# Sinkhorn's tiles summed before its product, one turn for the shares of two passes, and the first scalings on ScalarE

## The chip, the cores and the metric

The kernel runs on one core of one Trainium2 chip. The metric is the time of one execution on the device in microseconds; lower is better. The kernel before has a median of 2116.34 us over three runs (2116.13 to 2116.73).

## The reference

A local attention with a few global keys feeds a mixture of eight experts. Attention: batch 4, 8 heads, 768 positions, 64 columns a head; its output is read as x, 3072 tokens by 512 columns. The experts: layer one is 512 to 1024, layer two 1024 to 512, and every token passes through all eight. The weight P of each expert for each token is made by eight rounds of Sinkhorn:

```python
logits = x @ w_gate                       # 3072 x 8
P = np.exp(logits - logits.max())
for _ in range(8):
    P /= P.sum(1, keepdims=True) + 1e-09  # over the experts of a token
    P /= P.sum(0, keepdims=True) + 1e-09  # over all tokens, for each expert
    P *= N / E
for e in range(E):
    out += P[:, e:e + 1] * (np.maximum(x @ w1[e], 0.0) @ w2[e])
```

All is float32.

## The kernel before

**The stages.** First the attention, with a part of expert 0 computed in the background. Then pass 0 of the experts over the last third of the tokens (1024 of 3072, eight tiles of 128), in which the weights are prepared and written to DRAM as they are used; then passes 1 and 2 over the other two thirds, which read the prepared weights back. The cut falls near 264 us (end of attention) and 910 us (end of pass 0) of the profile.

**Pass 0** is a loop over 31 groups g of two 128-wide blocks of hidden units: three groups of expert 0 (its first block pair was done in the background), then four for each of experts 1 to 7. Each turn of the loop computes the first layer of group g (`layer1_strassen`, 42 products of 512 columns into the PSUM banks a, b, c, d), prepares the weights of a later group on ScalarE and GpSimd, and computes the second layer of group g - 1 (`second`, lines 1192 to 1213: eight tiles of 512 columns, six products each, in three PSUM banks `y_ps`). VectorE adds each tile into an accumulator `acc` (in the trace a part of the tile `early`): without a weight for expert 0 (line 1204), with the share P as a per-row scale for the others (line 1210). Before the first group of expert 1 is added, the eight accumulator tiles are multiplied by the share of expert 0: `first_scaled`, lines 1206 to 1209, four on VectorE (i = 1) and four on ScalarE (i = 0). This is done in the turn g = 4, for group 3.

**Sinkhorn** (`sinkhorn`, lines 913 to 943) works on `pm`, 128 partitions by 24 token tiles by 8 experts, so that a token is a partition and a tile. A round sums over the experts on VectorE (line 934), divides (935 to 937), and then needs a sum over all tokens: a product with a 128 x 128 matrix of ones sums over partitions for all 192 columns and spreads the result to every partition (line 939), and VectorE sums its 24 tiles from PSUM (line 940) before it divides (941 to 943). It is a generator, and `beat()`, called at places in the first and second layers, moves it on by one step, so that its products are traced between those of the first groups.

**The shares of passes 1 and 2.** There the tokens lie along the free dimension, so the share of an expert is needed as a row, spread over partitions. `spill_rows` (lines 1179 to 1185) turns the shares: in each of the turns g = 7, 8, 9 and 10 four transposes of a 128 x 8 block of `pm` go to one PSUM tile `pr_ps`, ScalarE copies 8 x 512 to `prow`, and a DMA writes it to `p_rows` in DRAM. `load_share` (line 1161) reads rows of it back, the first time near 900 us.

**What sets the order.** Each engine runs its instructions in a fixed order. A planner sets this order while the program is built, from its own estimate of when inputs and buffers are there: an instruction that is ready sooner may be issued ahead of ones traced before it. Instructions that go through `Ordered` or `InOrder` (lines 51 and 108) stay in the order of the program: TensorE from the turn g = 4 on (`moe.pe = attention.pe`, line 1242; all of those have line 115 or 118 in the profile), not before, and Sinkhorn's own products not. ScalarE's and SyncE's work in pass 0 is free from the turn g = 1 on.

Of the kernel before, what the change touches and what calls it, by code (L numbers as in the profile page):

```python
# [8 lines left out]
F32 = mybir.dt.float32  # L9
# [3 lines left out]
ALU = mybir.AluOpType  # L13
AX = mybir.AxisListType
# [3 lines left out]
P = 128  # L18
# [4 lines left out]
EPS = 1e-9  # L23
UT = 3
UNIT = UT * P
WT = 4
WIDE = WT * P
# [541 lines left out]
class Moe:  # L569
# [343 lines left out]
    def sinkhorn(self, ps, tag):  # L913

        nc, E, N = self.nc, self.E, self.N
        TT = N // P
        lg, pm, ones, small = self.lg, self.pm, self.ones, self.small
        gm = small.tile([P, 1], F32, name="gm")
        nc.vector.tensor_reduce(out=gm, in_=lg.rearrange("p t e -> p (t e)"), op=ALU.max, axis=AX.X)
        yield  # L920
        gmt_ps = ps.tile([P, P], F32, name="gmt_ps", tag=tag)
        self.pe.transpose(out=gmt_ps[0:1], in_=gm, identity=self.ident)
        gmax = small.tile([1, 1], F32, name="gmax")
        nc.vector.tensor_reduce(out=gmax, in_=gmt_ps[0:1], op=ALU.max, axis=AX.X)
        yield
        ngm_ps = ps.tile([P, 1], F32, name="ngm_ps", tag=tag)
        self.pe.matmul(ngm_ps, lhsT=ones[0:1, :], rhs=gmax, start=True, stop=True)
        nc.vector.tensor_scalar(out=gm, in0=ngm_ps, scalar1=-1.0, scalar2=None, op0=ALU.mult)
        nc.scalar.activation(out=pm, in_=lg, func=AF.Exp, bias=gm, scale=1.0)
        cols = TT * E  # L930
        for _ in range(SINKHORN_ITERS):
            bank = ps.tile([P, cols + TT + E], F32, name="c_ps", tag=tag)
            c_ps, rsum, csum = bank[:, 0:cols], bank[:, cols:cols + TT], bank[:, cols + TT:]
            nc.vector.tensor_reduce(out=rsum, in_=pm, op=ALU.add, axis=AX.X)
            nc.vector.tensor_scalar(out=rsum, in0=rsum, scalar1=EPS, scalar2=None, op0=ALU.add)
            nc.vector.reciprocal(out=rsum, in_=rsum)
            nc.vector.tensor_tensor(out=pm, in0=pm, in1=rsum.unsqueeze(2).broadcast_to([P, TT, E]), op=ALU.mult)
            yield
            self.pe.matmul(c_ps, lhsT=ones, rhs=pm, start=True, stop=True)
            nc.vector.tensor_reduce(out=csum, in_=c_ps.rearrange("p (t e) -> p e t", e=E), op=ALU.add, axis=AX.X)  # L940
            nc.vector.tensor_scalar(out=csum, in0=csum, scalar1=EPS, scalar2=float(E) / N, op0=ALU.add, op1=ALU.mult)
            nc.vector.reciprocal(out=csum, in_=csum)
            nc.vector.tensor_tensor(out=pm, in0=pm, in1=csum.unsqueeze(1).broadcast_to([P, TT, E]), op=ALU.mult)


def pipeline(tc, attention, ident, moe, acc, scratch):
# [4 lines left out]
    nc = tc.nc  # L951
    KT, KH, DM, NU, E = moe.KT, moe.KH, moe.DM, moe.NU, moe.E
    BT = 2 * WT
    NB = NU * UT // BT
# [4 lines left out]
    with ExitStack() as top:  # L959
# [9 lines left out]
        p_rows = dram.tile([E, NB - 1, 2, WIDE], F32, name="p_rows")  # L969
# [10 lines left out]
        NG = len(groups)  # L980
        xs = []
        for u in range(NU):
            c = u * UT % RT
# [109 lines left out]
        sps = first.enter_context(tc.tile_pool(name="sps", bufs=1, space=PSUM, reuse_waits="tile"))  # L1093
# [32 lines left out]
        def beat():  # L1126
            next(sinkhorn, None)
# [6 lines left out]
        passes = [NB - 1] + list(range(NB - 1))  # L1134
        FULL = DM // 2

        def spill_weights(g):

            w = wts[g]
            if g < NG - 1:  # L1140
                if g:
                    w2_sums[g] = w2pool.tile([P, 4, FULL], F32, name="w2sum", bufs=1)
                    moe.winograd_sums(w, w2_sums[g])
                t = moe.winograd_blocks(w2_sums[g], w2pool)
            to = w_spill[g] = dram.tile([P, 14, 2, FULL], F32R, name=f"ws{g}")
            dma(to[:, 0:7], w[0], sync if g == 0 else nc.sync)
            if g == NG - 1:
                for f in range(FG):
                    for s in range(2):
                        dma(to[:, 7 + 2 * f:9 + 2 * f, s], w[1][:, s, f].rearrange("p (d c) -> p d c", d=2))  # L1150
                return
            dma(to[:, 10], w[1][:, :, 1, 0:FULL])
            for d in range(2):
                dma(to[:, 12 + d], w[1][:, :, 0, d * FULL:(d + 1) * FULL])
            dma(to[:, 7:10], t[:, 0:3])
            dma(to[:, 11], t[:, 3])
# [19 lines left out]
                for m in range(lo, hi):  # L1176
                    blocks_of[0, 0, m] = t[:, m - lo]

        def spill_rows(p, i):

            bank = sps.tile([P, WT, P], F32, name="pr_ps", tag="s")
            for t in range(WT):
                moe.pe.transpose(out=bank[0:E, t], in_=moe.pm[:, passes[p + 1] * BT + 2 * t + i], identity=ident)
            nc.scalar.copy(out=prow[0:E], in_=bank[0:E].rearrange("p t c -> p (t c)"))
            nc.sync.dma_start(out=p_rows[:, p, i], in_=prow[0:E])

        def reload(p, ms=FIRST_BLOCKS):
            for m in ms:
# [3 lines left out]
        def second(g, hs, halves=(0, 1)):  # L1192
            e, b = groups[g][0], passes[0]
            first_scaled = e != 0 and groups[g - 1][0] == 0
            for i in halves:
                for t in range(WT):
                    j = 2 * t + i
                    tt = b * BT + j
                    y_ps = moe.layer2(t, wts[g], hs[i], yps, "y")
                    if t == 2:  # L1200
                        beat()
                    a = acc[:, j]
                    if e == 0:
                        nc.vector.tensor_tensor(out=a, in0=y_ps, in1=a, op=ALU.add)
                    else:
                        if first_scaled and i:
                            nc.vector.tensor_scalar(out=a, in0=a, scalar1=moe.pm[:, tt, 0:1], scalar2=None, op0=ALU.mult)
                        elif first_scaled:
                            nc.scalar.mul(a, a, moe.pm[:, tt, 0:1])
                        nc.vector.scalar_tensor_tensor(out=a, in0=y_ps, scalar=moe.pm[:, tt, e:e + 1], in1=a,  # L1210
                                                       op0=ALU.mult, op1=ALU.add)
                    if g == NG - 1:
                        nc.sync.dma_start(out=moe.out[tt * P:(tt + 1) * P, :], in_=a)

        for j in list(range(1, BT - UT, 2)) + list(range(0, BT - UT, 2)):
            u, t = divmod(passes[0] * BT + j, UT)
# [8 lines left out]
        def pieces_of_last(n):  # L1225
            for _ in range(n):
                next(last, None)
# [12 lines left out]
        for g in range(NG):  # L1240
            if prev is not None and groups[prev[0]][0] > 0:
                moe.pe = attention.pe
            to = ring_set if g == 0 else ring_set[0:2] + pool_set[2:4] if g == 1 else (pool_set, ring_set)[g % 2]
            hs = moe.layer1_strassen(ops, wts[g], to, tmp, mps, "h", g == 0, first_beat if g == 0 else beat)
            if g == 0:
                pieces_of_last(2 * UT)
                fill.close()
                w2pool = first.enter_context(tc.tile_pool(name="w2pool", bufs=2, side="right", reuse_waits="tile"))
                hpool = first.enter_context(tc.tile_pool(name="hpool", bufs=1))
                h_set = hpool.tile([P, 8, WIDE], F32R, name="h_set")  # L1250
                prow = hpool.tile([P, WIDE], F32, name="prow")
                pool_set += [(h_set[:, n], h_set[:, n + 1]) for n in range(0, 8, 2)]
                second(g, hs, (1,))
                moe.plain_blocks(wts[1])
            spill_weights(g)
            if g + 1 < NG and g + 1 not in wts:
                wts[g + 1] = moe.strassen_pair(moe.strassen_stage(*moe.stage_pair(*groups[g + 1], stage), stage),
                                               wpools[(g + 1) % 2])
                moe.plain_blocks(wts[g + 1])
            if 0 <= g - NG // 4 < 2 * (NB - 1):  # L1260
                spill_rows(*divmod(g - NG // 4, 2))
            if g == NG - 1:
                reload(1)
            if g == 1:
                second(*prev, (0,))
                second(g, hs, (0,))
                moe.act = nc.scalar
            elif g == 2:
                second(*prev, (1,))
            elif prev is not None:  # L1270
                second(*prev)
            prev = (g, hs)
# [146 lines left out]
def kernel(  # L1419
# [40 lines left out]
    with tc.If(rv > 0) as cmp:  # L1460
        pipeline(tc, band, ident, moe, acc, scratch)
# [34 lines left out]
```

## Time and profile before

| | us |
|---|---|
| median of three runs | 2116.34 (2116.13 to 2116.73) |
| the profiled execution, its own time | 2116.03 |
| span of its profile, first to last instruction | 2114.2 |
| TensorE busy | 2098.1 (99%) |
| GpSimd, VectorE, ScalarE busy | 1518.1, 1327.0, 725.6 |

The profile names engines PE (TensorE's products), PEld (its weight loads), DVE (VectorE), ACT (ScalarE), POOL (GpSimd) and SP (SyncE, which issues the DMAs). A row of a timeline has the start in us from the first instruction, the duration, the engine, the line of the kernel, the operation, output and inputs, shapes, count, and in brackets the idle time before and what ended it. The duration of one product includes the part in which the next already runs, so the pace of products is read from their starts.

### The profile page before, as it was taken

The page shows a single profiled execution, that of the slowest core. Times are in us where ns is not written, and L with a number is a line of the kernel's source. Part 1 is how long each engine was busy: PE and PEld are TensorE (multiplying, and loading weights), DVE is VectorE, ACT ScalarE, POOL GpSimd, SP SyncE. Part 2 cuts the span into 40 slices and gives each one's busy share as a digit, 9 for nine tenths or more (in the row PEclk, how much of TensorE's full clock was granted, in tenths as well). Part 3 has the DMA queues.
Part 4 walks back from the last instruction along what each step waited for, and adds up shares of the span by engine and source line. Part 5 has one row for each costly group of instructions (what it writes and reads, how often), then busy time and mean ns, then how long its engine had stood idle before and what let it go on. Part 6 is the DMA issues. An engine that isn't in the chain of part 4 may idle for free.

```text
span 2114.2 us, 30105 instructions
## 1 busy us (share of the span) xinstructions
PE 2098.1 (99%) x10505; PEld 1737.7 (82%) x10505; DVE 1327.0 (63%) x2368; ACT 725.6 (34%) x1487; POOL 1518.1 (72%) x1338
## 2 busy tenths in 40 slices
PE   8999999999999999999999999999999999999998
PEld 6888888888888888888888888888788888888886
DVE  7777667656566665655666556656746665566556
ACT  7777634323233332223222222222232222222221
POOL 5977969776777877347767677677577767777675
PEclk9999999999999999999999999999999999999999
DMA  7777487566666656776566565666956566566564
GB/s 168 211 208 207 145 298 295 217 235 223 240 235 223 244 214 244 246 281 210 184 213 208 187 209 182 218 206 218 357 186 208 185 211 212 177 204 212 189 207 149
DMA packets 235043, 458.04 MB, mean 217 GB/s; under 512 B 106465, under 2 KB 167905, under 8 KB 215169
## 3 DMA queue, kind: packets, MB, share of 16 engines
q1 hardware_dynamic: 234880, 456.01, 63.3%
q8 instruction: 85, 1.39, 0.3%
q14 instruction: 78, 0.63, 0.1%
HBM read 313.80 MB, written 142.15 MB: 216 GB/s over the span
## 4 chain that ended last, share of the span: by engine, by line
PE 94%; DVE 3%; POOL 1%; DMA 1%; issue 1%; ACT 0%; SPq 0%; DVEq 0%; ACTq 0%; POOLq 0%
PE c_acc L115 26%; PE y_ps L115 16%; PE bank_c L115 11%; PE bank_a L115 11%; PE bank_d L115 11%; PE bank_b L115 5%; PE t_ps L118 2%; PE o_ps L115 2%; PE s_ps L115 2%; PE h_ps L115 1%; PE o_t L115 1%; DVE early L1357 1%; PE tp L118 1%; PE y_ps L876 1%; PE y_ps L875 1%
## 5 line engine op out<-in xcount | busy, mean ns | idle before, releaser
L1353 DVE TENSOR_TENSOR early<-early,c_acc 128x512 f32<-128x512 f32 x308 | 210.2, 687 | 174.8 <-PE c_acc L115 174.8
L59 POOL TENSOR_TENSOR early<-full,full 128x512 f32<-128x512 f32 x56 | 72.8, 1300 | 291.0 <-DVE full L762 291.0
L59 POOL TENSOR_TENSOR full<-full,full 128x512 f32<-128x512 f32 x174 | 227.1, 1305 | 0.3
L1210 DVE SCALAR_TENSOR_TENSOR early<-y_ps,pm,early 128x512 f32<-128x512 f32 x224 | 167.5, 749 | 84.2 <-PE y_ps L115 83.9
L115 PE MATMUL bank_c<-x,wb 128*128 128x512 f32 x732 | 185.8, 389 | 0.0
L115 PE MATMUL bank_a<-m,wb 128*128 128x512 f32 x732 | 185.7, 389 | 0.0
L115 PE MATMUL bank_d<-x,wb 128*128 128x512 f32 x732 | 185.7, 389 | 0.0
L115 PEld LDWEIGHTS bank_a<-m,wb 128*128 128x128 f32 x732 | 137.4, 188 | 28.5
L115 PEld LDWEIGHTS bank_d<-x,wb 128*128 128x128 f32 x732 | 137.4, 188 | 28.5
L115 PEld LDWEIGHTS bank_c<-x,wb 128*128 128x128 f32 x732 | 137.4, 188 | 28.6
L115 PE MATMUL y_ps<-w,x 128*128 128x512 f32 x672 | 155.1, 389 | 0.6 <-DVE early L1210 0.6
L115 PE MATMUL y_ps<-w,h_set 128*128 128x512 f32 x672 | 154.8, 389 | 0.0
L115 PEld LDWEIGHTS y_ps<-w,x 128*128 128x128 f32 x672 | 125.9, 188 | 27.1 <-DVE early L1210 1.1
L115 PEld LDWEIGHTS y_ps<-w,h_set 128*128 128x128 f32 x672 | 126.0, 188 | 26.1
L773 DVE TENSOR_TENSOR early<-early,bank_d 128x512 f32<-128x512 f32 x62 | 42.6, 687 | 152.5 <-PE bank_d L115 152.3
L115 PE MATMUL c_acc<-x,wb 128*128 128x512 f32 x540 | 137.0, 389 | 0.0
L622 POOL TENSOR_TENSOR w<-w1f,w 128x256 fp32r<-128x256 f32 x62 | 44.9, 743 | 122.0 <-ACT w L621 122.0
L115 PEld LDWEIGHTS c_acc<-x,wb 128*128 128x128 f32 x540 | 101.3, 188 | 21.1
L643 POOL TENSOR_TENSOR wsum<-w1f 128x256 f32<-128x256 f32 x155 | 109.4, 741 | 9.1 <-DMA w1f<-in_moe_w_dram 9.1
L59 POOL TENSOR_TENSOR x<-full,x 128x512 fp32r<-128x512 f32 x90 | 115.9, 1324 | 0.0
L765 ACT CAST x<-full 128x512 fp32r<-128x512 f32 x90 | 56.0, 623 | 161.9 <-POOL full L59 135.9
L359 ACT ACTIVATE p_sb<-p_sb,mx 128x256 f32<-128x256 f32 (+1 forms) x192 | 92.5, 483 | 41.0 <-DVE mx L355 40.4
(375 smaller groups left out, 5063.4 us busy)
## 6 DMA issues: line engine op xcount, KB each, us to landing
wb<-ws SPq DMA_DIRECT2D x123, 1024.0 KB, 6.7
wb<-ws SPq DMA_DIRECT2D x121, 768.0 KB, 4.2
ws<-w SPq DMA_DIRECT2D x31, 1792.0 KB, 5.7
ws<-w SPq DMA_DIRECT2D x94, 256.0 KB, 2.5
ws<-w2s SPq DMA_DIRECT2D x30, 768.0 KB, 5.3
w1f<-in_moe_w_dram SPq DMA_DIRECT2D x32, 512.0 KB, 4.1
w2f<-in_moe_w_dram SPq DMA_DIRECT2D x32, 512.0 KB, 4.5
x<-op_m SPq DMA_DIRECT2D x16, 512.0 KB, 9.5
```

The costliest lines, as they stand in the source:

```text
L59: return lambda *args, **kw: self.tc.keep_in_program_order(op(*args, **kw))
L115: return self.tc.keep_in_program_order(self.engine.matmul(*args, **kw))
L118: return self.tc.keep_in_program_order(self.engine.transpose(*args, **kw))
L359: nc.scalar.activation(out=pv, in_=pv, func=AF.Exp, bias=mx[:, u:u + 1], scale=-1.0, accum_out=sm[:, i, j:j + 1])
L622: self.nc.gpsimd.tensor_tensor(out=lo, in0=full, in1=hi, op=ALU.subtract)
L643: nc.gpsimd.tensor_tensor(out=s[:, n], in0=x, in1=y, op=op)
L765: nc.scalar.copy(out=ops[k][:, 0], in_=src)
L773: tt(out=t3, in0=t3, in1=d, op=ALU.subtract)
L875: self.pe.matmul(y_ps, lhsT=hh[:, cols], rhs=lf, start=(f == 0), stop=False)
L876: self.pe.matmul(y_ps, lhsT=hl[:, cols], rhs=wf, start=False, stop=False)
L1210: nc.vector.scalar_tensor_tensor(out=a, in0=y_ps, scalar=moe.pm[:, tt, e:e + 1], in1=a, op0=ALU.mult, op1=ALU.add)
L1353: nc.vector.tensor_tensor(out=sums[k][q], in0=sums[k][q], in1=bank, op=ALU.add)
```

## The change

1. In each round of Sinkhorn VectorE sums the 24 tiles first, from SBUF, into a new tile `part` of 128 x 8. The product with the ones then has 8 columns and not 192, and the division reads its result from PSUM directly; the sum that stood behind the product is gone. The number of VectorE instructions is the same.
2. `spill_rows` is called once, in the turn g = 7. Two ScalarE copies bring the shares of both passes into a new tile `pcol`, 128 x 128, in the order (expert, pass, half, tile); one transpose of 128 x 128 turns them, one ScalarE copy of 128 x 128 takes them to `prow`, and one DMA writes all 128 rows. Before there were 16 transposes, four copies and four DMAs in four turns.
3. All eight first scalings go to ScalarE.

```diff
@@ sinkhorn @@
-        cols = TT * E
+        part = small.tile([P, E], F32, name="c_part")
         for _ in range(SINKHORN_ITERS):
-            bank = ps.tile([P, cols + TT + E], F32, name="c_ps", tag=tag)
-            c_ps, rsum, csum = bank[:, 0:cols], bank[:, cols:cols + TT], bank[:, cols + TT:]
+            bank = ps.tile([P, TT + 2 * E], F32, name="c_ps", tag=tag)
+            c_ps, rsum, csum = bank[:, 0:E], bank[:, E:E + TT], bank[:, E + TT:]
             nc.vector.tensor_reduce(out=rsum, in_=pm, op=ALU.add, axis=AX.X)
             nc.vector.tensor_scalar(out=rsum, in0=rsum, scalar1=EPS, scalar2=None, op0=ALU.add)
             nc.vector.reciprocal(out=rsum, in_=rsum)
             nc.vector.tensor_tensor(out=pm, in0=pm, in1=rsum.unsqueeze(2).broadcast_to([P, TT, E]), op=ALU.mult)
+            nc.vector.tensor_reduce(out=part, in_=pm.rearrange("p t e -> p e t"), op=ALU.add, axis=AX.X)
             yield
-            self.pe.matmul(c_ps, lhsT=ones, rhs=pm, start=True, stop=True)
-            nc.vector.tensor_reduce(out=csum, in_=c_ps.rearrange("p (t e) -> p e t", e=E), op=ALU.add, axis=AX.X)
-            nc.vector.tensor_scalar(out=csum, in0=csum, scalar1=EPS, scalar2=float(E) / N, op0=ALU.add, op1=ALU.mult)
+            self.pe.matmul(c_ps, lhsT=ones, rhs=part, start=True, stop=True)
+            nc.vector.tensor_scalar(out=csum, in0=c_ps, scalar1=EPS, scalar2=float(E) / N, op0=ALU.add, op1=ALU.mult)
...
@@ pipeline @@
-        def spill_rows(p, i):
-
-            bank = sps.tile([P, WT, P], F32, name="pr_ps", tag="s")
-            for t in range(WT):
-                moe.pe.transpose(out=bank[0:E, t], in_=moe.pm[:, passes[p + 1] * BT + 2 * t + i], identity=ident)
-            nc.scalar.copy(out=prow[0:E], in_=bank[0:E].rearrange("p t c -> p (t c)"))
-            nc.sync.dma_start(out=p_rows[:, p, i], in_=prow[0:E])
+        def spill_rows():
+
+            row = pcol.rearrange("q e p i t -> q (e p i t)")
+            for p in range(NB - 1):
+                first_tile = passes[p + 1] * BT
+                nc.scalar.copy(out=pcol[:, :, p], in_=moe.pm[:, first_tile:first_tile + BT].rearrange("q (t i) e -> q e i t", i=2))
+            bank = sps.tile([P, P], F32, name="pr_ps", tag="s")
+            moe.pe.transpose(out=bank, in_=row, identity=ident)
+            nc.scalar.copy(out=prow, in_=bank)
+            nc.sync.dma_start(out=p_rows.rearrange("e p i (t c) -> (e p i t) c", c=P), in_=prow)
...
-                        if first_scaled and i:
-                            nc.vector.tensor_scalar(out=a, in0=a, scalar1=moe.pm[:, tt, 0:1], scalar2=None, op0=ALU.mult)
-                        elif first_scaled:
+                        if first_scaled:
                             nc.scalar.mul(a, a, moe.pm[:, tt, 0:1])
...
-                prow = hpool.tile([P, WIDE], F32, name="prow")
+                prow = hpool.tile([P, P], F32, name="prow")
+                pcol = hpool.tile([P, E, NB - 1, 2, WT], F32, name="pcol")
...
-            if 0 <= g - NG // 4 < 2 * (NB - 1):
-                spill_rows(*divmod(g - NG // 4, 2))
+            if g == NG // 4:
+                spill_rows()
```

## The prediction, made before the result was known

> **What bounds the kernel now.** I read the engines' totals first, then TensorE's own waits in the stretch that the change touches, then that stretch turn by turn, then single rows. The totals and the chain of waits:
>
> ```profile
> PE 2098.1 (99%) x10505; PEld 1737.7 (82%) x10505; DVE 1327.0 (63%) x2368; ACT 725.6 (34%) x1487; POOL 1518.1 (72%) x1338
> ...
> PE 94%; DVE 3%; POOL 1%; DMA 1%; issue 1%; ACT 0%; SPq 0%; DVEq 0%; ACTq 0%; POOLq 0%
> ```
>
> TensorE is busy for 99% of the span and is 94% of the chain that ends last. So an edit pays only in TensorE time that it takes away, or in a wait of TensorE that it ends. In 255 to 520 us, where all of the change lies, the list of TensorE's waits has one row:
>
> ```profile
> PE y_ps L115 <- DVE early L1210: 0.6, 1, 0.6
> ```
>
> The stretch in windows, each one turn of the loop (columns: window, length, busy time and instructions of each engine, granted clock, DMA share, GB/s):
>
> ```profile
> 345.95:367.66 21.71, 21.07 (x94) 17.14 (x93) 16.75 (x27) 8.96 (x14) 18.94 (x19) 1.00 0.74 288
> ...
> 388.06:408.46 20.40, 20.40 (x92) 16.90 (x91) 12.55 (x18) 6.64 (x10) 15.39 (x15) 1.00 0.62 231
> 408.46:429.34 20.88, 20.88 (x96) 17.17 (x95) 12.64 (x18) 7.10 (x11) 15.87 (x15) 1.00 0.63 237
> 429.34:450.20 20.86, 20.86 (x96) 17.16 (x95) 12.64 (x18) 7.10 (x11) 15.38 (x15) 1.00 0.65 228
> 450.20:471.07 20.87, 20.87 (x96) 17.16 (x95) 12.58 (x18) 7.11 (x11) 15.46 (x15) 1.00 0.62 228
> 471.07:491.93 20.86, 20.86 (x96) 17.16 (x95) 12.59 (x18) 7.10 (x11) 15.37 (x15) 1.00 0.63 227
> ```
>
> A turn with nothing of the change in it is 20.40 us: 90 products, 0.2267 each. The four turns with transposes are 20.88 + 20.86 + 20.87 + 20.86 = 83.47, which is 1.87 above four plain turns. The turn from 345.95 is 1.31 above one; it holds the last round of Sinkhorn and the wait. These excesses, and seven more rounds of Sinkhorn before 345.95, are all that the change can win on TensorE.
>
> **Part 1, the product of 8 columns.** What a round costs now, from starts on TensorE (the last two rows are the weight loads behind the pair; all float32 products here are two instructions):
>
> ```profile
> 281.60 0.39 PE L710 MATMUL bank_a<-m,w 128*128 128x512 f32 x1
> 281.82 0.49 PE L939 MATMUL c_ps<-pm,ones 128*128 128x192 f32 x2
> 281.99 0.19 PEld L708 LDWEIGHTS bank_c<-x,w 128*128 128x128 f32 x1
> 282.15 0.19 PEld L709 LDWEIGHTS bank_c<-x,w 128*128 128x128 f32 x1
> 282.38 0.40 PE L709 MATMUL bank_c<-x,w 128*128 128x512 f32 x1
> ```
>
> From 281.60 to 282.38 TensorE does one product of 512 columns, the pair, and another such product; less 2 x 0.2267 the pair takes 0.33. A weight load is issued when the product before it begins, so the loads at 281.99 and 282.15 put each half at 0.165. Eight rounds are 8 x 0.33 = 2.6.
>
> No row shows a full-width pair of 8 columns. The nearest:
>
> ```profile
> 262.47 0.35 PE L907 MATMUL gt_ps<-ident,g_sb 16*128 16x16 f32 x3
> 262.75 0.19 PEld L710 LDWEIGHTS h_ps<-x,w1h 128*128 128x128 f32 x1
> 262.86 0.19 PEld L708 LDWEIGHTS h_ps<-x,w1h 128*128 128x128 f32 x1
> ...
> 276.35 0.38 PE L927 MATMUL ngm_ps<-gmax,ones 1*128 1x1 f32 x2
> 276.66 0.50 PE L890 MATMUL y_ps<-w2h,hh 128*128 128x512 f32 x1
> ```
>
> Three products of 16 columns take 262.75 - 262.47 = 0.28, so 0.093 each, and the weight load behind them, with no long product to hide it, holds the array for 262.86 - 262.75 = 0.11. A pair of one column takes 276.66 - 276.35 = 0.31. So weights decide, not columns: behind a product of 8 columns the next load lies bare. The first load of a pair still hides behind a product of 512, the second and that of the next product do not: 2 x 0.11 = 0.22. I take that, since the 16-column row is nearest in width: saved 0.33 - 0.22 = 0.11 a round, 0.9 in all. Bounds: the one-column pair (0.02 a round, 0.2 in all) and a pair that costs nothing (2.6).
>
> [...]
>
> On VectorE a round keeps its eight instructions; one sum moves ahead of the product:
>
> ```profile
> L934 DVE TENSOR_REDUCE c_ps<-pm x8: 349/360/363, 277.9 to 343.9; 128x24 f32<-128x192 f32 x8
> L937 DVE TENSOR_TENSOR pm<-pm,c_ps x8: 343/353/355, 279.3 to 345.6; 128x192 f32<-128x192 f32 x8
> L940 DVE TENSOR_REDUCE c_ps<-c_ps x8: 353/356/367, 282.3 to 350.9; 128x8 f32<-128x192 f32 x8
> ```
>
> The sum removed is 0.356; the new one, from SBUF, is closest to line 934, 0.360 (with a stride, so perhaps a little more). That it lies ahead of the product costs nothing: the first division ends at 279.3 + 0.35 = 279.65 and its product starts at 281.82, 2.2 later; the last ends at 345.95, its product is the 16th of that row, after 350. TensorE never waited for one. Were that cover gone, it would be 8 x 0.36 = 2.9.
>
> **Part 2, one turn for the shares.** 1.87 over 16 transposes is 0.117 each. The new one has 128 columns of weights and not 8; the nearest row is eight transposes of the attention with a product behind them:
>
> ```profile
> 251.16 1.09 PE L118 MATMUL t_ps<-ident,p_sb 128*128 128x128 f32 x8
> ...
> 252.01 0.48 PE L115 MATMUL y_ps<-w2l,hh 128*128 128x512 f32 x1
> ```
>
> (252.01 - 251.16) / 8 = 0.106 each, so wide weights are no dearer. One alone, with its change to and from the other products, I take as 0.15: saved 1.72 (bounds 1.6 and 1.77). Fifteen transposes, three DMA issues on SP and a copy less; p_rows is not read before 900 us, so neither the later single DMA nor its smaller rows lie on anything.
>
> What is added is a wait: the transpose needs two ScalarE copies, where the old ones needed only pm. Behind it on TensorE, in program order, are the 48 products of the second layer. When ScalarE does the copies is the planner's choice:
>
> ```profile
> 397.69 0.71 ACT L621 CAST w<-w1f 128x256 fp32r<-128x256 f32 x2
> 409.88 0.59 ACT L845 COPY early<-bank_c 128x512 f32<-128x512 f32 x1 [0.26 <-PE bank_c L115]
> ...
> 420.82 0.58 ACT L715 ACTIVATE x<-bank_a 128x512 fp32r<-128x512 f32 x1
> 421.31 1.04 ACT L679 CAST w2s<-w2sum 128x1024 fp32r<-128x1024 f32 x1
> ...
> L929 ACT ACTIVATE pm<-lg,gm x1: 457/457/457, 277.3 to 277.3; 128x192 f32<-128x192 f32 x1
> ```
>
> The casts at 397.69 are traced after the whole first layer of the turn that begins at 408.46 (they prepare weights of g = 8), yet run as soon as their buffer is free, ahead of line 845 of that layer. So the copies, which need only pm, should run soon after Sinkhorn ends near 353, over 60 us early. Cost nothing; without that cover, below.
>
> **Part 3, the scalings.** The wait of TensorE, with what leads to it:
>
> ```profile
> 352.78 3.78 DVE L1207 TENSOR_SCALAR early<-early,pm 128x512 f32<-128x512 f32 x4
> 356.49 0.68 DVE L716 SCALAR_TENSOR_TENSOR h_set<-bank_b,h_set 128x512 fp32r<-128x512 f32 x1
> ...
> 359.79 1.40 DVE L1210 SCALAR_TENSOR_TENSOR early<-y_ps,pm,early 128x512 f32<-128x512 f32 x2
> ...
> 355.70 4.24 PE L115 MATMUL y_ps<-w,x 128*128 128x512 f32 x18
> 360.58 5.74 PE L115 MATMUL y_ps<-w,x 128*128 128x512 f32 x24 [0.64 <-DVE early L1210]
> ...
> 353.02 2.55 ACT L1209 ACTIVATE early<-early,pm 128x512 f32<-128x512 f32 x4
> 357.79 0.60 ACT L715 ACTIVATE h_set<-bank_d 128x512 fp32r<-128x512 f32 x1 [1.13 <-DVE early L858]
> L1207 DVE TENSOR_SCALAR early<-early,pm x4: 473/720/2102, 352.8 to 356.1; 128x512 f32<-128x512 f32 x4
> ```
>
> The four scalings hold VectorE for 3.78; the rest of the first layer comes after, and the first y_ps bank is free only at 360.5. TensorE, which has three such banks, finishes 18 products at 355.70 + 18 x 0.2267 = 359.78 and goes on at 360.58, 0.80 later. By the window it is 1.31 - 0.33 = 0.98, by the trace's own idle 0.64; I take 0.9. Without the 3.78 VectorE reaches the first y_ps tile when it is there, about 357.3 (six products and the drain), and is done by 358.7 even with one other operation ahead: 1.1 before it is needed. ScalarE has eight scalings at 2.55 / 4 = 0.64, 5.1 in all, until 358.1 or a little later with other work between; a new one is needed every 1.36 from 357.3, and the fifth is done by 356.3. Saved 0.9 (bounds 0 and 0.98).
>
> [...]
>
> **Sum.** 0.9 + 1.7 + 0.9 = 3.5. The profiled execution took 2116.03 (span 2114.2 and 1.8 around it), so 2112.5 for it; the median is 0.3 above that one, so 2112.8. A measurement of this kernel can tell about 0.2% from no change, 4.2 us: the sum falls a little short of it.
>
> **The rivals.**
>
> (a) Weight loads hide after all: both loads of the ones are pulled ahead behind the product of 512, and a pair costs nearly nothing. Part 1 then saves up to 2.6 and the time is 2111.1. For it: the first load does hide (the pair starts on time at 281.82). Against: the bare load of 0.11 at 262.75. [...]
>
> (b) The wait at 360 stays in another form: with eight scalings ahead of it on ScalarE, line 715 for bank d runs at 358.1 to 358.7, line 716 behind it to 359.4, and if VectorE still has that ahead of the first line 1210, the bank comes free at 360.1, not 360.5. Only 0.4 or nothing is won in part 3: 2113.3 to 2113.7. Against: in the old order other ScalarE work slips between, since it is ready first. A pair of 8 columns at the one-column price (0.31) gives the same 2113.5.
>
> (c) Slower: the two copies stand on ScalarE behind the first layer of g = 7. Its last operation there starts at 421.31 and ends at 422.35; two copies of some 0.45 (the exponential of 192 columns, line 929, takes 0.457) bring 423.3, and the transpose, which could start at 417.84, holds back TensorE for 5.4. Less 3.5 won, 2118.2. It decides as soon as the copies end after 421.4 (a wait over 3.5). Against: the casts at 397.69.
>
> (d) The planner gives TensorE, free before turn g = 4, another order between 264 and 346, where no wait of it is listed now; it can hardly win there, and a few waits like that of line 1210 cost 1 to 5: 2114 to 2118.
>
> **How the numbers follow.** Forecast 52%, (a) 17%, (b) 15%, (c) 5%, (d) 11%. The forecast's own range is 2111.5 to 2114. The range of 8 in 10 takes in (a) with part 1 at its bound, (b), and the lower part of (d): 2110.2 to 2116.2. Faster by over 0.2% means below 2112.1: most of (a), 0.15, and two fifths of the forecast, 0.21: 0.36. Slower means above 2120.6: only (c) or (d) beyond their prices, 0.06. The rest, 0.58, is within.
>
> **What would show it.** Part 1: starts on TensorE around a c_ps pair 0.22 apart beyond the plain pace. Part 2: the turns from 429 to 492 at 20.40, that from 408 at 20.55. Part 3: no row of TensorE waiting for line 1210, the turn from 346 at 20.6. It is wrong if TensorE waits for a pr_ps or c_ps input, or if the turns before 346 change in length by more than the pairs do.

## The result, and the profile after

The changed kernel takes 2138.62 us (median of 5 runs, 2138.31 to 2138.93) where the kernel before took 2116.34 (2116.01 to 2117.02) beside it: a ratio of 1.0105, with a 95% interval of 1.0094 to 1.0116. It is 22.3 us slower; the forecast was 3.5 us less. The profiled execution took 2138.31.

The span and the engines' totals of the changed kernel:

```profile
span 2136.5 us, 30083 instructions
PE 2121.1 (99%) x10490; PEld 1735.4 (81%) x10490; DVE 1326.6 (62%) x2364; ACT 725.8 (34%) x1490; POOL 1518.7 (71%) x1338
```

TensorE is busy 23 us longer with 15 instructions fewer; its weight loads (PEld) take 2.3 us less, and no other engine moved by over 1 us. In 255 to 520 us TensorE's list of waits is empty: the one wait of before is gone, and no new one came. That points to the products themselves. The window 500 to 910 us, in which nothing of the change is executed, first in the kernel before, then in the changed one:

```profile
500.00:910.00 410.00, 410.00 (x1811) 339.60 (x1810) 253.05 (x363) 126.37 (x190) 278.42 (x249) 1.00 0.65 238
```

```profile
500.00:910.00 410.00, 410.00 (x1763) 330.62 (x1762) 246.90 (x355) 126.38 (x191) 279.19 (x249) 1.00 0.62 228
```

TensorE is busy throughout in both, at the full granted clock, and gets 48 products less done. Where these are slower shows the chain of waits (start, length, what). The kernel before, one bank of six products and the second layer of a turn:

```profile
408.48 1.36 PE bank_c L115 x6
...
603.47 10.88 PE y_ps L115 x48
```

The changed kernel, two starts of a turn, parts of another turn of pass 0, and then a stretch of pass 1:

```profile
367.47 1.40 PE bank_c L115 x6
...
388.42 1.40 PE bank_c L115 x6
...
544.96 11.20 PE y_ps L115 x48
556.16 1.40 PE bank_c L115 x6
557.55 1.40 PE bank_d L115 x6
558.96 1.39 PE bank_a L115 x6
560.35 1.36 PE bank_b L115 x6
...
1049.52 1.36 PE bank_c L115 x6
1050.88 1.36 PE bank_d L115 x6
1052.24 1.40 PE bank_a L115 x6
1053.64 1.40 PE bank_b L115 x6
1055.04 1.39 PE bank_c L115 x6
...
1057.79 1.40 PE bank_a L115 x6
1059.19 10.90 PE c_acc L115 x48
```

There are two paces and little between them: 10.88 / 48 = 1.36 / 6 = 0.2267 a product, and 11.20 / 48 = 1.40 / 6 = 0.2333, 6.7 ns more. In pass 0 all products run at or near the slow one but those of bank b; in pass 1 it is those of banks a and b (and the six behind b, 1.39), while bank d and the second layer, c_acc, are fast. A turn of pass 0 is 20.95 (from 367.47 to 388.42) where it was 20.40. Marks of the chain say where the 22 us went; before, then after (the last tiles of pass 0, the first c_acc of pass 1 and its last, the same of pass 2):

```profile
889.07 21.76 PE y_ps L115 x96
...
934.84 7.12 PE c_acc L115 x30
...
1464.23 7.50 PE c_acc L115 x33
...
1534.14 7.09 PE c_acc L115 x30
...
2063.47 7.50 PE c_acc L115 x33
```

```profile
901.16 22.40 PE y_ps L115 x96
...
947.72 7.09 PE c_acc L115 x30
...
1481.88 7.52 PE c_acc L115 x33
...
1551.66 7.09 PE c_acc L115 x30
...
2085.82 7.52 PE c_acc L115 x33
```

Pass 0 ends 12.7 later (910.83 to 923.56), pass 1 adds 1481.88 - 1464.23 - (947.72 - 934.84) = 4.8, pass 2 again 4.8.

### The profile page after: what moved, and what is told of

Its sections match the earlier page's. It is cut to its first block, busy times and chain, and to the rows that moved or that the text cites. A ratio compares the mean times of both kernels' runs of the same rounds, so it can differ in the third digit from the quotient of the medians.

```text
span 2136.5 us, 30083 instructions
## 1 busy us (share of the span) xinstructions
PE 2121.1 (99%) x10490; PEld 1735.4 (81%) x10490; DVE 1326.6 (62%) x2364; ACT 725.8 (34%) x1490; POOL 1518.7 (71%) x1338
## 3 DMA queue, kind: packets, MB, share of 16 engines
q8 instruction: 85, 1.39, 0.3%
## 4 chain that ended last, share of the span: by engine, by line
PE 95%; DVE 2%; issue 1%; POOL 1%; ACT 0%; DMA 0%; DVEq 0%; SPq 0%; ACTq 0%; POOLq 0%
PE c_acc L115 26%; PE y_ps L115 16%; PE bank_a L115 11%; PE bank_c L115 11%; PE bank_d L115 11%; PE bank_b L115 6%; PE t_ps L118 2%; PE o_ps L115 2%; PE s_ps L115 2%; PE h_ps L115 1%; PE tp L118 1%; PE o_t L115 1%; PE y_ps L875 1%; PE y_ps L876 1%; PE y_ps L877 1%
## 5 line engine op out<-in xcount | busy, mean ns | idle before, releaser
L115 PE MATMUL bank_a<-m,wb 128*128 128x512 f32 x732 | 190.8, 396 | 0.0
L115 PE MATMUL y_ps<-w,h_set 128*128 128x512 f32 x672 | 159.2, 396 | 0.0
```

The lines of the kernel that those rows point to most:

```text
L115: return self.tc.keep_in_program_order(self.engine.matmul(*args, **kw))
```

## The experiments

**What moved.** The change adds a tile, part, 8 floats a partition, to the pool of constants, which lies below everything that the passes allocate from the bottom of the memory. So all of those tiles begin 32 bytes further up in the built program; the tiles allocated from the top stay. From the bottom come x (a ring of buffers, which in pass 0 also takes the first layer's results of every second group), h_set (which takes those of the others), and the weights of passes 1 and 2 (wb) with most of their operands; from the top the weights of pass 0 (w1, w2) and the operands m1, m6 and m7. In pass 1 of the changed kernel the products of banks c and d and of c_acc take both operands from the bottom: these go at 0.2267, but for the six behind bank b. Theory A: a product is slower when its two operands, the stationary and the moving one, begin at different places within some block of bytes. Theory B: the planner's new order, or the new instructions, make them slower.

The runs on this are made from either kernel by sizes alone:

```diff
after_pad64, after_pad128, after_pad256 (from the changed kernel; n = 2, 4, 8):
-        part = small.tile([P, E], F32, name="c_part")
+        part = small.tile([P, n * E], F32, name="c_part")[:, 0:E]
before_left32 (from the kernel before; half1 is not used by anything):
-        nc.gpsimd.memset(const.tile([P, 16], F32, name="half1"), 0.0)
+        nc.gpsimd.memset(const.tile([P, 24], F32, name="half1"), 0.0)
after_right32 and before_right32 (edge is the first tile from the top, filled with zeros and not read):
-    edge = ... .tile([P, 24], F32, name="edge")
+    edge = ... .tile([P, 16], F32, name="edge")
after_inplace (from the changed kernel; self.spare is the tile half1):
-        part = small.tile([P, E], F32, name="c_part")
+        part = self.spare[:, 0:E]
```

> The kernel before with one number altered: the unused tile half1 is 24 floats and not 16, so that the tiles behind it (the operands x, the buffers of the first layer's result and of the weights of passes 1 and 2) move by 32 bytes a partition, as in the changed kernel. No instruction of the change is in it. Theory A: as slow as the changed kernel plus what its three parts win, 2138.6 + 3.5 = 2142, with 48 y_ps products at 11.20 us. Theory B: 2116.3.

> The changed kernel with the unused tile edge at 16 floats and not 24: edge lies at the top, and all tiles allocated from the top (weights of pass 0, the operands m1, m6, m7) now also move by 32 bytes, so that both operands of nearly every product are 32 bytes off a 64-byte boundary. Theory A1 (what counts is that the two operands of a product lie at the same place within 64 bytes): fast again, about 2112.8, 48 y_ps products at 10.88. Theory A2 (every operand off the boundary costs by itself): 2138.6 or more, since more operands are off it; also passes 1 and 2, where the trace of the changed kernel has both operands off by 32 and a pace of 10.90, would then have been slow already. Theory B: 2138.6.

> The kernel before with edge at 16 floats: only the tiles from the top move by 32 bytes. Theory A1: in pass 0 the same pairs of operands differ as in the changed kernel, in passes 1 and 2 the products with m1, m6, m7 too: about 2142, as before_left32. Theory A2: slow in pass 0 (the weights are an operand of every product there), and in passes 1 and 2 only where m1, m6, m7 are read: some 2130 to 2142. Theory B: 2116.3.

> The changed kernel with one number altered: the new tile part is 64 bytes a partition wide (16 floats, of which 8 are used), not 32, so that every tile allocated behind it moves by 64 bytes against the kernel before and not by 32. The work is the same. Theory A (addresses: products got slower because tiles moved by 32 bytes): the pace of 48 y_ps products returns from 11.20 to 10.88 us and the time is what the three parts are worth alone, 2112.8 by the prediction's sum, within 2111.5 to 2114. Theory B (the planner's new order, or the new instructions themselves, slow the products): unchanged, about 2138.6.

> The changed kernel with part 128 bytes a partition wide, so the tiles behind it move by 128 bytes. By 64 bytes the time was 2137.0, so the block within which the operands have to agree is larger than 64 bytes. If it is 128 bytes: 2112.4 and 48 y_ps products at 10.88. If it is 256 or more: about 2137 and 11.20.

> The same with 256 bytes. If the block is 128 or 256 bytes: 2112.4. If it is larger, or if it isn't a block at all but the plain distance from the old place that counts: about 2137.

> The changed kernel with part put into the first 8 floats of the tile half1, which is there and unused, so that no tile lies elsewhere than in the kernel before; the three parts are as in the change. Theory A1 (the operands of a product must lie at the same place within some block): 2112.4, as with both sides moved by 32 bytes, 48 y_ps products at 10.88 us, no wait of TensorE for VectorE in 255 to 520 us. If the move of both sides itself had a price or a gain, it differs from 2112.4 by that. Theory B (new order or new instructions) fell with the run that moved both sides, and would have 2137 here.

All of them in one table. The places are those of the built programs, as the byte within 256 at which the tiles from the bottom and from the top begin:

| kernel | from the bottom | from the top | us, median | ratio to before |
|---|---|---|---|---|
| before | 128 | 128 | 2116.3 | |
| changed | 160 | 128 | 2138.62 | 1.0105 (1.0094 to 1.0116) |
| before_left32 | 160 | 128 | 2141.21 | 1.0120 (1.0103 to 1.0137) |
| before_right32 | 128 | 160 | 2141.78 | 1.0120 (1.0103 to 1.0137) |
| after_right32 | 160 | 160 | 2112.45 | 0.9983 (0.9973 to 0.9992) |
| after_pad64 | 192 | 128 | 2136.96 | 1.0098 (1.0081 to 1.0115) |
| after_pad128 | 0 | 128 | 2134.58 | 1.0085 (1.0066 to 1.0103) |
| after_pad256 | 128 | 128 | 2112.05 | 0.9980 (0.9970 to 0.9990) |
| after_inplace | 128 | 128 | 2112.27 | 0.9980 (0.9971 to 0.9989) |

Theory B is gone: the kernel before, with one unused tile made larger, is slow (2141.21, 2142 expected), and the changed kernel with everything moved alike is fast. Within theory A it is not the place of an operand by itself: with both sides at 160 the time is 2112.45. My first guess of the block, 64 bytes, was wrong: a move by 64 left the time at 2136.96 where I had written 2112.8, and 128 did not bring it back either; 256 did. So all nine rows fit one rule, both operands at the same place within 256 bytes. Distances other than 32, 64, 128 and 256 were not tried. Product by product it holds as well: in passes 1 and 2 of the changed kernel the starts of the products of banks a and b, whose operands lie at 128 and 160, are 0.2336 apart in the mean, and those of bank d, with both at 160, 0.2267. The second layer in after_pad64 and in after_right32:

```profile
607.35 11.20 PE y_ps L115 x48
```

```profile
600.52 10.88 PE y_ps L115 x48
```

**One operand of some products.** The last of these runs moves the contents of a single tile of after_inplace, the one that is the stationary operand in the second layer of every second group (of what lies behind it, prow and pcol move along; the one transpose reads pcol, and no other product reads either):

```diff
-                h_set = hpool.tile([P, 8, WIDE], F32R, name="h_set")
+                h_set = hpool.tile([P, 8 * WIDE + 8], F32R, name="h_set")[:, 8:].rearrange("p (n c) -> p n c", c=WIDE)
```

> The kernel of after_inplace with one edit: the tile h_set, which holds the first layer's result of every second group and gives the stationary operand (weights) of that group's y_ps products, begins 32 bytes later; no other operand moves. Theory A1 (a product is slow when its own two operands lie at different places within 256 bytes): in pass 0 only the y_ps products with h_set, and a few behind them, go at 11.20 us for 48, those with the ring's x stay at 10.88, passes 1 and 2 stay as they are; 15 groups by 0.32 and a little for the products behind, 2112.3 + 5 = 2117. If it is the order of the two sides as wholes, or something that the whole program has (code, DMA), that makes the difference, then no such alternation: either 2112.3, or all turns slow.

It took 2117.30 (ratio to before 1.0005, 0.9995 to 1.0014), 5.0 more than after_inplace; its lowest time, 2116.82, lies above the highest of that, 2112.78. The tile is an operand of 744 products, and 744 x 6.7 ns is 5.0. Its chain of waits, two turns:

```profile
601.83 10.88 PE y_ps L115 x48
612.71 1.36 PE bank_c L115 x6
...
620.87 1.37 PE bank_a L115 x6
622.24 11.20 PE y_ps L115 x48
633.44 1.36 PE bank_c L115 x6
...
642.96 10.88 PE y_ps L115 x48
```

The slow pace comes and goes with the tile, every second turn, and the groups of six between are at 1.36 or 1.37. So it is a matter of the products' own operands, and not of the program as a whole.

**The parts one by one**, with no operand moved, each from the kernel before:

```diff
part1_only: sinkhorn as in the change, part in the tile half1
part2_only: spill_rows, prow, pcol and the call as in the change
part3_only: the branch "if first_scaled and i" taken out, as in the change
```

> The kernel before with part 1 alone (the tiles summed ahead of the product of 8 columns), part lying in the unused tile half1 so that nothing moves. By the prediction's term 0.9 less than before, 2115.3 (0.2 to 2.6 less by its bounds). In the trace a pair should add 0.22 to the pace of TensorE, against 0.33; if weight loads hide, near 0. The wait for line 1210 stays.

> The kernel before with part 2 alone (one transpose of 128 x 128 for the shares), no tile moved that an operand of a product lies in. The prediction's term: 1.7 less, 2114.7, the turns that had transposes at 20.40, the first of them at 20.55, no wait for pr_ps or pcol; the wait for line 1210 stays. Rival (c) of the prediction: the copies to pcol come late on ScalarE, TensorE waits up to 5.4 for them and the time is 2120.

> The kernel before with part 3 alone (all eight first scalings on ScalarE), no tile moved. The prediction's term: 0.9 less, 2115.5, no wait of TensorE for line 1210 in the list of waits, and the turn that holds the last round of Sinkhorn at 20.40 + 0.33 and some after-effect, 20.75. Part 1 alone had no such wait either, so with both parts the 0.9 is won once only. Rival: eight scalings hold up ScalarE's other work, the wait stays in part, 2116.4.

| kernel | us, median | ratio to before | the profile's span (before 2114.2) |
|---|---|---|---|
| part1_only | 2114.27 | 0.9989 (0.9980 to 0.9999) | 2112.8 |
| part2_only | 2114.26 | 0.9991 (0.9982 to 1.0001) | 2112.2 |
| part3_only | 2114.79 | 0.9993 (0.9983 to 1.0003) | 2113.3 |
| after_inplace, all three | 2112.27 | 0.9980 (0.9971 to 0.9989) | 2110.4 |

Two of the intervals reach 1, so for the single parts the traces decide. The spans add up to 1.4 + 2.0 + 0.9 = 4.3, the three together give 3.8. The wait for line 1210 ended in part1_only too, where I had expected it to stay: it stands in two of the three terms and is won once. The turn that holds the wait and the last round of Sinkhorn tells whether it is there: 21.71 before, 366.00 - 345.34 = 20.66 in part1_only, and in part2_only, by its chain,

```profile
345.89 1.36 PE bank_c L115 x6
...
367.41 1.36 PE bank_c L115 x6
```

21.52. So in part2_only the wait stayed, as expected, although its list of waits has no row in 255 to 520 us: an empty list alone doesn't show that TensorE never waited. The turn with the one transpose is 20.56 there too (408.21 to 428.77), the next 20.40, and rival (c) did not come. VectorE in part1_only:

```profile
352.89 2.72 DVE L1208 TENSOR_SCALAR early<-early,pm 128x512 f32<-128x512 f32 x4
...
357.04 0.70 DVE L862 TENSOR_TENSOR bank_a<-bank_a,early 128x512 f32<-128x512 f32 x1
357.64 0.74 DVE L1211 SCALAR_TENSOR_TENSOR early<-y_ps,pm,early 128x512 f32<-128x512 f32 x1
```

The four scalings take 2.72, not 3.78, and the planner put the first y_ps tile (here line 1211) directly behind line 862 and ahead of line 717 for bank d, so the first bank is free at 358.4; which of the two ends the wait was not told apart. In part3_only the same tile is done at 358.2, and the turn with the last round is 366.81 - 346.03 = 20.78 (20.75 expected).

## Why the prediction was wrong

**The step that failed.** The prediction took the pace of a plain product, 0.2267, as a constant of the kernel, and argued that the excesses over it were all that the change could win; what the change could lose on TensorE it looked for only in waits and in the order of the work. It costed the instructions of part 1 and left out what `small.tile` does: the new tile is a further 32 bytes in front of the operands, so that most products of pass 0 and those of two banks in passes 1 and 2 go at 0.2333. None of the rivals had this. The slow pace costs 2138.62 - 2112.27 = 26.4 us, some 16.5 of it before the end of pass 0 (12.7 and the 3.8 that the parts win) and 4.8 in each later pass, and the forecast of the rest drowns in it. Two of the signs that the prediction named show it: the turns from 429 to 492 should have been 20.40 and are 20.95, and from the first pair of Sinkhorn to the turn g = 4 the time grew from 64.15 (281.82 to 345.97) to 64.53 (281.77 to 346.30), though seven pairs in it became shorter.

**Part 1, right.** The pair of 8 columns in after_inplace, by starts on TensorE:

```profile
281.65 0.39 PE L711 MATMUL bank_a<-m,w 128*128 128x512 f32 x1
281.88 0.28 PE L941 MATMUL c_ps<-half,ones 128*128 128x8 f32 x2
281.99 0.19 PEld L709 LDWEIGHTS bank_c<-x,w 128*128 128x128 f32 x1
282.10 0.19 PEld L710 LDWEIGHTS bank_c<-x,w 128*128 128x128 f32 x1
282.33 0.40 PE L710 MATMUL bank_c<-x,w 128*128 128x512 f32 x1
```

282.33 - 281.65 less 2 x 0.2267 is 0.23, where 0.22 was forecast; the loads behind the pair come 0.11 apart, each bare, as the step had it, so rival (a) fell. Read so, the eight pairs add 1.81 and those of the kernel before 2.68: 0.87 won, 0.9 forecast. That the sum over tiles lies ahead of the product cost TensorE no wait that a view shows, though the new sum was taken too low: 0.54 and not 0.36, in the changed kernel

```profile
L938 DVE TENSOR_REDUCE c_part<-pm x8: 528/540/570, 279.6 to 346.9; 128x8 f32<-128x192 f32 x8
```

**Part 2, right.** In after_inplace:

```profile
406.44 1.36 PE bank_c L115 x6
...
416.07 10.93 PE y_ps L115 x48
427.00 1.36 PE bank_c L115 x6
...
447.40 1.36 PE bank_c L115 x6
```

The turn with the one transpose is 427.00 - 406.44 = 20.56, the next 20.40; the four turns win 83.47 - 20.56 - 3 x 20.40 = 1.71, forecast 1.72. The copies it waits for ran long before, with the scalings:

```profile
351.92 5.02 ACT L1211 ACTIVATE early<-early,pm 128x512 f32<-128x512 f32 x8
356.84 0.50 ACT L1185 COPY pcol<-pm 128x64 f32<-128x64 f32 x2
357.25 0.59 ACT L716 ACTIVATE h_set<-bank_d 128x512 fp32r<-128x512 f32 x1
```

They end at 357.3, 58 us before the transpose: the planner issued them early, as argued from the casts, and rival (c) fell.

**Part 3, right in its size, too narrow in its cause.** The eight scalings take 5.02 on ScalarE (5.1 forecast), the wait is gone (the turn is 20.65) and TensorE pays nothing for it; line 716 for bank d does stand behind all eight, as rival (b) feared, but VectorE takes the first y_ps tile ahead of it. The wait hung on less than I thought: part 1 ended it alone, while the scalings were still on VectorE. One scaling takes 3.78 / 4 = 0.95 us in the mean on VectorE in the kernel before and 2.72 / 4 = 0.68 in part1_only; on ScalarE it takes 5.02 / 8 = 0.63 in after_inplace, where the prediction took 0.64.

**The sum.** With the tiles where they were, the change is worth 2116.43 - 2112.27 = 4.2 us by the medians of runs taken side by side (3.8 by the spans), forecast 3.5, and the predicted 2112.8 would have stood. The chain of after_inplace has it by stretches: the turn g = 4 begins 0.98 sooner than before (0.77 was forecast, seven pairs by 0.11), takes 365.64 - 344.99 = 20.65 and so 1.06 less (1.01: a pair and the wait), and the four turns with the shares 1.71 less (1.72).

```profile
344.99 1.36 PE bank_c L115 x6
...
365.64 1.36 PE bank_c L115 x6
```

Rival (d) did not come: the stretch ahead of that turn got shorter, and the list of waits has no row.

## What to carry to other kernels

A tile added is also a move of all that is allocated behind it (here by 32 bytes a partition, for 26.4 us): before costing the instructions of a change, list which operands it moves, and put small new tiles where nothing lies behind them, into space that is already there. When products of one shape are a little slower (here by 6.7 ns each) and nothing waits, compare the places of their operands before looking at the order of the work; one unused tile resized in the kernel before tells the two apart.

The version to keep is after_inplace, the change with part in the unused tile: 2112.27, faster than both.

## What the runs showed of the hardware

The products of the second layer of pass 0, 128 x 128 weights by 512 columns, go at 0.2267 us (10.88 for 48) where their two operands begin at the same byte within 256, in the kernel before and in after_right32; at 0.2333 (11.20 for 48) where they differ by 32 or 64, in the changed kernel and in after_pad64; and at 0.2324 (11.15 to 11.16) where they differ by 128, in after_pad128. That it hangs on their own operands is shown by the one tile of hset32, 11.20 against 10.88 in every second turn. What in the chip does it is open. So is a remainder: some products whose operands were not moved against each other took longer than 1.36 for six where they followed products whose operands were. In pass 0 of the changed kernel the six products of bank a take 1.39, though both their operands lie at the top; they follow the slow products of bank d. In pass 1 the six of bank c behind the slow bank b take 1.39, and in after_pad128 even those of bank b take 1.38 in pass 0:

```profile
559.68 1.38 PE bank_b L115 x6
...
565.24 11.16 PE y_ps L115 x48
```

But behind the slow y_ps products of hset32 bank c is at once at 1.36. No run here separates these.
